# Linear attention and MLP in one kernel: the first block's reciprocals all transposed by DMA, in a new order of all engines

## The chip, the cores and the metric

The kernel runs on one core of a Trainium2 chip. The metric is the device time of one execution in microseconds (us); lower is better. A profile shows one execution: TensorE matmuls (PE) and weight loads (PEld), VectorE (DVE), ScalarE (ACT), GpSimd (POOL), and the queue of SyncE (SP or SPq), which issues every data transfer of this kernel.

## The reference

`x` is 2048 rows by 512 columns in bf16. An attention block with 32 heads of 16 and a two-layer MLP follow each other, each behind a layer norm and each added to its input:

```python
qkv = _layernorm(x) @ wqkv                       # 512 -> 3*512
phi = lambda t: jnp.where(t > 0, t + 1, jnp.exp(t)) + 1e-6
kv  = jnp.einsum("bhsd,bhse->bhde", phi(k), v)   # per head, over all rows
z   = jnp.einsum("bhsd->bhd", phi(k))
num = jnp.einsum("bhqd,bhde->bhqe", phi(q), kv)
den = jnp.einsum("bhqd,bhd->bhq", phi(q), z)[..., None] + 1e-6
h   = x + (num / den) @ wo
h2  = h + relu(_layernorm(h) @ w1) @ w2          # 512 -> 1792 -> 512
```

## The kernel before

The rows are cut into 16 tiles of 128, and four tiles make a block of 512 rows (blocks 0 to 3). A text, ORDER, lists every step of the kernel as a word, such as `K.8.0`. The words are issued one after the other, and each engine executes its own words in that order; semaphores are set from what each word reads and writes. So a word's place decides what it stands behind on its engine, and nothing is rescheduled later. The last number of a PE word is mostly the bank of the accumulator `bk` (8 banks) that it writes.

The words that matter, with their lines in the kernel before:

- `lx`, `lk`, `lq`, `lv`, `lo`, `l1`, `l2` (L201, L204): loads of the input and of the weights, issued by SP. `l1` and `l2` move 896 KB each.
- `S`, `A`, `R`, `N` (L222 to L250): layer norm of an input tile into `h_nat`, on DVE, with `R` (two activations) on ACT. `T` and `E` (L266, L276): transposing tiles 0 to 3 on PE and copying them to `lnT` on ACT. `X` (L287): transposing the other tiles by a DMA that SP issues.
- `K`, `Q` (L295, L303): the k and q products, four matmuls each. `F`, `U`, `M`, `D` (L313, L316, L320, L323): exp and relu on ACT, minimum and sum on DVE, which make phi. `W` (L328) takes the place of `U` and `D`: one DVE instruction that reads the accumulator itself. `qF` ... `qW` are the same for q.
- `G` (L347): a tile's share of phi(k) transposed times the normed input, into four banks; after 16 tiles `gA` (ACT, L380) or `gD` (DVE, L383) copy them to `gT`. `z`, `zc`, `zh`: the sums over phi(k). `kv`, `kx`, `m`, `mA` (L388 to L403): the product with the v weights, the mask, the product with `wo`.
- `dn` (L444): the denominators of a block, 16 small matmuls. `dnl` (L450) and `dnx` (L457): logarithm and exp(-x) on ACT, which give the reciprocals by row in `rn` (the buffer of the k weights, `wk_sb`, once these are used up).
- `dt` (L476): a reciprocal tile transposed by DMA into `rd`. `rt` and `re` (L266, L468): the same by four PE transposes and a copy on ACT. In the kernel before, tile 3 goes by `rt.3.3` and `re.3`, and all other tiles by `dt`.
- `dm` (L480): phi(q) times reciprocals into `pqs`, on DVE, one word for half a block. It needs all four tiles of the block's `rd`; and the `dt` of the next block, which write the same `rd`, wait for both `dm` words of this one.
- `h`, `hD`, `s`, `a`, `n` (L490, L496, L224, L225, L254): attention output of a tile, residual, second layer norm. `x` (L288): that tile transposed by DMA into `lnT`.
- `p`, `pA`, `pD` (L506, L512, L517): first MLP product and relu on ACT or DVE; each `p` word reads all four tiles of its block's `lnT`. `f`, `fo`, `fd` (L526, L534, L541): second MLP product, scaling with residual, store.

All DMAs share one queue and eight semaphores in turn: each DMA waits until the one eight places ahead of it has landed.

Of the kernel before, what the change touches and what calls it, by code (L numbers as in the profile page):

```python
# [15 lines left out]


ORDER = """
const table lx.0.1 lx.2.1 S.0 lx.1.1 S.2 A.0 S.1 A.2 R.0.1 N.0 R.2.1 lx.3.1 lk.0.2 lx.4.2 warm.1.7 warm.9.7
A.1 R.1.1 T.0.6 S.3 N.2 N.1 A.3 E.0 lk.2.2 warm.1.7 R.3.1 S.4 T.2.7 lx.6.2 E.2 N.3 S.5 T.1.4 A.4 K.0.1 E.1 A.5  # L20
F.0.1 R.4.2 S.6 T.3.2 K.1.0 M.0.1 E.3 U.0.1 lx.8.4 K.2.3 F.1.1 N.5 masks U.1.1 N.4 S.7 D.0.1 M.1.1 A.7 A.6
R.6.2 D.1.1 K.3.2 F.2.1 F.3.1 U.2.1 U.3.1 S.9 N.6 lx.12.4 X.5 G.0 X.4 G.1 M.2.1 A.9 S.8 N.7 A.8 M.3.1 D.2.1
R.8.2 K.5.1 lq.0.2 D.3.1 N.9 K.4.0 F.4.2 X.6 S.13 N.8 X.7 G.2 A.13 S.12 M.4.2 X.9 A.12 G.3 U.4.2 R.12.2 K.6.2
X.8 D.4.2 K.7.3 N.12 S.10 S.11 N.13 G.4 K.9.1 K.8.0 F.6.2 U.6.2 A.11 M.6.2 A.10 X.12 R.10.2 D.6.2 X.13 N.11
S.15 N.10 A.15 za.2 U.8.2 F.8.2 S.14 M.8.2 A.14 G.5 G.6 G.7 X.11 K.12.0 X.10 K.13.1 K.11.3 R.14.2 lq.2.2 za.4
N.14 D.8.2 K.10.2 N.15 za.6 X.14 F.12.2 U.12.2 X.15 F.10.2 G.8 Q.0.0.0 Q.0.1.1 M.12.2 lv.2.2 l1.0.2 l1.2.2
lo.0.4 lv.0.2 U.10.2 K.14.2 G.9 K.15.3 D.12.2 M.10.2 za.8 D.10.2 qU.0.0.2 G.10 za.10 qF.0.0.2 F.14.2 qM.0.0.2
za.12 Q.0.2.0 Q.0.3.1 G.11 M.14.2 zf.12 qF.0.2.2 G.12 W.14.2 qM.0.2.2 l2.7.7 qD.0.0.2 G.13 z.1.2.14 z.3.2.14
z.2.2.14 z.0.2.14 zc qW.0.2.2 G.14 G.15 zh dn.0.0 dnl.0 dnx.0.0.2 gD.2.2 gD.0.2 Q.1.0.2 Q.1.1.3 Q.1.3.1 kv.2.4
kv.3.4 dnx.0.3.1 dnx.0.2.1 kv.1.4 kv.0.4 Q.1.2.0 kx qF.1.0.2 qU.1.0.2 m.0.4 rt.3.3 m.2.6 m.1.5 Q.2.0.2 m.3.7  # L30
dt.1 qM.1.0.2 qF.1.2.2 dt.0 dt.2 re.3 qD.1.0.2 Q.2.1.3 mA.0.2 qM.1.2.2 l2.0.7 mA.2.2 qW.1.2.2 dn.1.5 dm.0.0.2
Q.2.3.1 dnl.1 dnx.1.0.2 dm.0.2.2 h.3.5 hD.3 dnx.1.2.2 qF.2.0.2 qU.2.0.2 s.3 h.1.4 hD.1 a.3 s.1 h.0.5 Q.2.2.0
n.3 hD.0 dt.5 dt.6 h.2.4 qU.2.2.2 qF.2.2.2 a.1 s.0 dt.7 hD.2 n.1 s.2 a.0 n.0 dt.4 dm.1.0.2 Q.3.0.2 Q.3.1.3
Q.3.3.1 Q.3.2.0 dm.1.2.2 a.2 x.3 h.4.6 h.7.4 qU.3.0.2 qF.3.0.2 x.1 h.6.5 h.5.7 qF.3.2.2 n.2 qM.2.2.2 qM.2.0.2
qD.2.0.2 qM.3.0.2 qD.2.2.2 x.0 dn.2.3 x.2 dnl.2 dnx.2.2.2 p.0.0.2 p.0.1.3 hD.4 qM.3.2.2 qW.3.2.2 qD.3.0.2
pD.0.0.2 hD.7 hD.5 dnx.2.0.2 p.0.3.1 dn.3.6 p.0.2.0 dt.10 dt.11 hD.6 s.5 s.4 dt.8 dt.9 p.0.5.3 p.0.4.2
dm.2.2.2 s.7 a.7 dm.2.0.2 r.0.4 pA.0.2.2 dnl.3 pA.0.4.2 p.0.7.1 p.0.6.0 dnx.3.2.2 pA.0.6.2 p.0.13.3 f.0.4.0.7
p.0.12.2 pA.0.12.2 f.1.5.0.7 h.9.3 h.10.1 h.11.0 h.8.6 dnx.3.0.2 a.4 s.6 hD.9 a.5 a.6 hD.10 hD.11 p.0.9.3
p.0.11.1 p.0.8.2 p.0.10.0 dt.14 dt.13 dt.15 f.3.7.0.7 pA.0.10.2 pA.0.8.2 n.5 dt.12 n.6 dm.3.0.2 dm.3.2.2 n.4
s.11 n.7 hD.8 h.14.1 h.13.3 f.0.4.7.7 h.12.0 h.15.6 hD.14 s.10 s.8 s.14 hD.12 s.9 x.5 x.7 x.6 x.4 f.1.5.7.7  # L40
f.3.7.7.7 fo.0 hD.15 p.1.9.1 p.1.8.0 f.2.6.0.7 pA.1.8.2 f.2.6.7.7 p.1.0.0 p.1.1.1 fo.1 a.14 a.10 a.8 fo.3 s.12
a.11 a.12 s.15 a.15 n.11 hD.13 s.13 a.13 a.9 n.8 n.10 p.1.3.3 n.9 n.12 pA.1.0.2 fo.2 x.10 fd.3 x.9 x.8 x.11
p.1.10.6 p.1.4.0 p.1.7.5 fd.0 p.1.5.1 p.1.2.2 p.1.11.7 p.1.6.4 n.14 pD.1.6.2 r.12.4 pA.1.4.2 n.15 n.13
pD.1.10.2 pA.1.2.2 p.2.4.0 p.2.5.1 pA.2.4.2 x.15 f.5.5.0.7 p.2.0.0 p.2.1.1 p.2.2.2 p.2.3.3 pA.2.0.2 p.1.13.1
f.7.7.0.7 p.1.12.0 f.4.4.0.7 pD.2.2.2 pD.1.12.2 p.2.7.3 p.2.6.2 p.2.13.1 f.6.6.0.7 f.7.7.7.7 f.5.5.7.7
p.2.12.0 r.4.4 pD.2.6.2 p.2.10.2 f.6.6.7.7 pA.2.12.2 x.12 x.14 x.13 fd.1 fd.2 p.2.9.1 p.2.11.3 p.2.8.0 fo.7
pA.2.10.2 pD.2.8.2 f.4.4.7.7 p.3.3.3 p.3.9.1 p.3.8.0 fo.4 pA.3.8.2 fo.5 fo.6 f.8.4.0.7 p.3.5.1 p.3.4.0 p.3.2.2
f.9.5.0.7 pD.3.4.2 pD.3.2.2 fd.5 fd.4 p.3.0.0 f.10.6.0.7 f.9.5.7.7 f.10.6.7.7 p.3.6.2 p.3.7.3 p.3.1.1 fd.6
f.8.4.7.7 pD.3.6.2 pA.3.0.2 r.8.4 fo.9 fo.10 p.3.13.1 f.11.7.0.7 p.3.11.3 p.3.12.0 pA.3.12.2 fo.8 f.11.7.7.7
fd.7 fd.9 p.3.10.2 f.12.4.0.7 f.14.6.0.7 fo.11 pD.3.10.2 f.15.5.0.14.3.1 f.12.4.7.7 f.14.6.7.7 fd.8 fd.10  # L50
fd.11 fo.15.3.1 fo.12 fo.14 f.13.5.0.7 f.13.5.7.7 fo.13 f.15.7.0.14.0.2 fd.12 fd.14 fd.13 fd.15.3.1
f.15.4.0.14.2.1 fo.15.0.2 fd.15.0.2 fo.15.2.1 fd.15.2.1
"""


# [521 lines left out]
```

## Time and profile before

| what | value |
|---|---|
| median of 3 runs | 170.41 us (170.32 to 170.6) |
| the profiled execution | 171.34 us |
| its span in the trace | 169.6 us |
| granted TensorE clock | 1.0 |

The profiled execution is 0.93 us above the median, and 1.74 us of it lie outside the span. The span is what the views of the trace divide; a saving in it is taken over to the median as it stands.

### The profile page before, as it was taken

Reading aid. Unit: us, or ns where it says so; the run is one execution under the profiler, and the core shown is the slowest. Engines: PE = TensorE matmul, PEld = TensorE weight load, DVE = VectorE, ACT = ScalarE, POOL = GpSimd, SP = SyncE. Lnnn points to the kernel's source line nnn. Section 1 sums busy time; section 2 is a strip of 40 time slices with the busy share of each in tenths; the row PEclk is TensorE's granted clock in tenths of the full one; section 3 lists DMA queues with packets and bytes.
Section 4 is the critical chain, followed back from the end, with each engine's and each line's share of the span. In section 5 each row is a group of like instructions: output and inputs, shape, how many; then the busy total and the mean of one; then the engine's idle time right before and its main releaser. Section 6 shows DMA issues by size and latency. Waiting matters only on the chain.

```text
span 169.6 us, 2272 instructions
## 1 busy us (share of the span) xinstructions
PE 162.6 (96%) x847; PEld 75.6 (45%) x863; DVE 102.6 (61%) x203; ACT 65.2 (38%) x98; POOL 4.9 (3%) x21
## 2 busy tenths in 40 slices
...
GB/s 128 312 192 142 110 81 125 270 395 261 65 122 203 108 64 66 62 31 95 60 69 0 9 115 62 69 120 1 0 0 0 124 0 4 0 93 31 0 66 62
DMA packets 31675, 15.75 MB, mean 93 GB/s; under 512 B 24240, under 2 KB 30640, under 8 KB 31664
## 3 DMA queue, kind: packets, MB, share of 16 engines
...
q8 instruction: 7, 0.11, 0.3%
q14 instruction: 4, 0.03, 0.1%
HBM read 7.86 MB, written 2.10 MB: 59 GB/s over the span
## 4 chain that ended last, share of the span: by engine, by line
PE 83%; DMA 7%; DVE 5%; SPq 2%; issue 2%; ACT 0%; DVEq 0%
PE bk L526 28%; PE bk L506 28%; PE bk L490 9%; PE bk L303 6%; PE bk L347 6%; PE bk L295 4%; DMA x_nat<-in_A_x_dram 3%; DMA lnT<-h_nat 2%; DVE st L222 2%; DMA rd<-wk_sb 2%; SPq L201 1%; DVE h_nat L247 1%; DVE eb L320 1%; PE bk L444 1%; PE bk L388 1%
## 5 line engine op out<-in xcount | busy, mean ns | idle before, releaser
L526 PE MATMUL bk<-w_sb,at 128*128 128x512 bf16 (+2 forms) x248 | 51.2, 355 | 0.2
L506 PE MATMUL bk<-lnT,w_sb 128*128 128x512 bf16 x220 | 50.9, 380 | 0.2
L512 ACT ACTIVATE at<-bk 128x1024 bf16<-128x1024 f32 x17 | 17.2, 1022 | 67.3 <-PE bk L506 60.9
L526 PEld LDWEIGHTS <-at 128*128 128x128 bf16 x252 | 23.5, 98 | 25.2
L506 PEld LDWEIGHTS <-w_sb 128*128 128x128 bf16 x224 | 21.7, 98 | 26.0
L517 DVE TENSOR_SCALAR at<-bk 128x1024 bf16<-128x1024 f32 x11 | 13.4, 1223 | 32.7 <-PE bk L506 32.6
L534 DVE SCALAR_TENSOR_TENSOR gT<-bk,rstd,h_nat 128x512 bf16<-128x512 f32 (+2 forms) x18 | 12.0, 688 | 15.9 <-PE bk L526 14.8
L313 ACT ACTIVATE eb<-bk 128x1024 bf16<-128x1024 f32 (+1 forms) x18 | 16.4, 924 | 4.0 <-PE bk L295 2.4
L295 PE MATMUL bk<-wk_sb,lnT 128*128 128x512 bf16 x63 | 15.3, 380 | 0.7 <-DMA lnT<-h_nat 0.5
L490 PE MATMUL bk<-m_sb,pqs 128*128 128x512 bf16 x61 | 15.1, 380 | 0.2
L303 PE MATMUL bk<-lnT,wq_sb 128*128 128x512 bf16 x61 | 14.6, 379 | 0.1
L496 DVE TENSOR_TENSOR h_nat<-bk,x_nat 128x512 bf16<-128x512 f32 x16 | 10.8, 684 | 4.7 <-PE bk L490 4.7
L316 ACT ACTIVATE rb<-bk 128x1024 bf16<-128x1024 f32 (+1 forms) x14 | 12.5, 901 | 2.6 <-PE bk L303 1.9
L347 PE MATMUL bk<-at,h_nat 128*128 128x512 bf16 x56 | 13.4, 379 | 0.1
L222 DVE BATCH_NORM_STATS2 st<-x_nat 128x6 f32<-128x512 bf16 x16 | 10.7, 677 | 3.1 <-DMA x_nat<-in_A_x_dram 3.1
L224 DVE BATCH_NORM_STATS2 st<-h_nat 128x6 f32<-128x512 bf16 x16 | 10.7, 682 | 0.1
L347 PEld LDWEIGHTS <-h_nat 128*128 128x128 bf16 x64 | 6.2, 98 | 8.7 <-issue 1.5
L490 PEld LDWEIGHTS <-pqs 128*128 128x128 bf16 x64 | 5.9, 98 | 8.7 <-DVE pqs L480 2.0
L295 PEld LDWEIGHTS <-lnT 128*128 128x128 bf16 x64 | 6.0, 98 | 8.3 <-DMA lnT<-h_nat 1.4
L303 PEld LDWEIGHTS <-wq_sb 128*128 128x128 bf16 x64 | 6.1, 97 | 6.9
L457 ACT ACTIVATE wk_sb<-ld 128x1024 bf16<-128x1024 f32 (+1 forms) x9 | 8.2, 951 | 0.1
L480 DVE TENSOR_TENSOR pqs<-pqT,rd 128x1024 bf16<-128x1024 bf16 x8 | 5.2, 685 | 4.4 <-DMA rd<-wk_sb 2.6
...
## 6 DMA issues: line engine op xcount, KB each, us to landing
w_sb<-in_B_w_dram SPq DMA_DIRECT2D x4, 896.0 KB, 5.8
...
```

The source lines that it names most:

```text
L222: op_S = lambda t: nc.vector.bn_stats(out=st[:, t, :], in_=x_nat[:, t, :])
L295: nc.tensor.matmul(bk[:, b, :], lhsT=lnT[c][:, kd, j * P : (j + 1) * P], rhs=wk_sb[:, kd, :], start=(kd == 0), stop=(kd == KD - 1),)
L303: nc.tensor.matmul(bk[:, b, :], lhsT=wq_sb[:, kd, j * P : (j + 1) * P], rhs=lnT[c][:, kd, :], start=(kd == 0), stop=(kd == KD - 1),)
L313: nc.scalar.activation(out=buf(eb, kind, i, n), in_=bank(at_bank[kind, i], n), func=ACT.Exp)
L316: nc.scalar.activation(out=buf(rb, kind, i, n), in_=bank(at_bank[kind, i], n), func=ACT.Relu)
L347: nc.tensor.matmul(bk[:, KD + kd, :], lhsT=ln_nat[:, t, kd * P : (kd + 1) * P], rhs=pk(t)[:, 0, :], start=(t == 0), stop=(t == NT - 1),)
L490: nc.tensor.matmul(bk[:, b, :], lhsT=pqs[:, (c * KD + jb) % NQ, j * P : (j + 1) * P], rhs=m_sb[:, jb, :], start=(jb == 0), stop=(jb == KD ...
L506: nc.tensor.matmul(bk[:, b, cols], lhsT=w1_sb[:, kd, f * P : (f + 1) * P], rhs=lnT[c][:, kd, cols], start=(kd == 0), stop=(kd == KD - 1),)
L512: nc.scalar.activation(out=acts[c % 2][:, f : f + n, :], in_=bank(at_bank["p", c, f], n), func=ACT.Relu)
L517: nc.vector.tensor_scalar(out=acts[c % 2][:, f : f + n, :], in0=bank(at_bank["p", c, f], n), scalar1=0.0, scalar2=None, op0=ALU.max,)
L526: nc.tensor.matmul(bk[:, b, 0 : w * P], lhsT=acts[c % 2][:, f, j * P : (j + 1) * P], rhs=w2_sb[:, f, k * P : (k + w) * P], start=(f == 0), ...
L534: nc.vector.scalar_tensor_tensor(out=o_t[:, t % NO, cols], in0=bk[:, at_bank["f", t, k], 0 : w * P], scalar=rstd2[:, t : t + 1], in1=h_nat ...
```

## The change

The set of computations is the same. The words differ in these points:

- `rt.3.3` and `re.3` are gone, and `dt.3` is added: all four reciprocal tiles of block 0 go by DMA. The two words `dnx.0.3.1` and `dnx.0.2.1` become one, `dnx.0.2.2`.
- `W.14.2` becomes `U.14.2` and `D.14.2`; `qW.0.2.2` becomes `qU.0.2.2` and `qD.0.2.2`; `gD.0.2` becomes `gA.0.2`; `lv.2.2` and `lv.0.2` become one load `lv.0.4`.
- Fourteen relu words change sides, eight from DVE to ACT (`pD.0.0.2` becomes `pA.0.0.2`) and six from ACT to DVE, and many `T`, `K` and `h` words get another bank.
- All the rest is order. A new function, `op_warmq`, is defined, and no word calls it.

The diff, cut to the first third of the order and the new function:

```diff
-const table lx.0.1 lx.2.1 S.0 lx.1.1 S.2 A.0 S.1 A.2 R.0.1 N.0 R.2.1 lx.3.1 lk.0.2 lx.4.2 warm.1.7 warm.9.7
-A.1 R.1.1 T.0.6 S.3 N.2 N.1 A.3 E.0 lk.2.2 warm.1.7 R.3.1 S.4 T.2.7 lx.6.2 E.2 N.3 S.5 T.1.4 A.4 K.0.1 E.1 A.5
-F.0.1 R.4.2 S.6 T.3.2 K.1.0 M.0.1 E.3 U.0.1 lx.8.4 K.2.3 F.1.1 N.5 masks U.1.1 N.4 S.7 D.0.1 M.1.1 A.7 A.6
-R.6.2 D.1.1 K.3.2 F.2.1 F.3.1 U.2.1 U.3.1 S.9 N.6 lx.12.4 X.5 G.0 X.4 G.1 M.2.1 A.9 S.8 N.7 A.8 M.3.1 D.2.1
-R.8.2 K.5.1 lq.0.2 D.3.1 N.9 K.4.0 F.4.2 X.6 S.13 N.8 X.7 G.2 A.13 S.12 M.4.2 X.9 A.12 G.3 U.4.2 R.12.2 K.6.2
-X.8 D.4.2 K.7.3 N.12 S.10 S.11 N.13 G.4 K.9.1 K.8.0 F.6.2 U.6.2 A.11 M.6.2 A.10 X.12 R.10.2 D.6.2 X.13 N.11
...
-za.12 Q.0.2.0 Q.0.3.1 G.11 M.14.2 zf.12 qF.0.2.2 G.12 W.14.2 qM.0.2.2 l2.7.7 qD.0.0.2 G.13 z.1.2.14 z.3.2.14
-z.2.2.14 z.0.2.14 zc qW.0.2.2 G.14 G.15 zh dn.0.0 dnl.0 dnx.0.0.2 gD.2.2 gD.0.2 Q.1.0.2 Q.1.1.3 Q.1.3.1 kv.2.4
-kv.3.4 dnx.0.3.1 dnx.0.2.1 kv.1.4 kv.0.4 Q.1.2.0 kx qF.1.0.2 qU.1.0.2 m.0.4 rt.3.3 m.2.6 m.1.5 Q.2.0.2 m.3.7
-dt.1 qM.1.0.2 qF.1.2.2 dt.0 dt.2 re.3 qD.1.0.2 Q.2.1.3 mA.0.2 qM.1.2.2 l2.0.7 mA.2.2 qW.1.2.2 dn.1.5 dm.0.0.2
-Q.2.3.1 dnl.1 dnx.1.0.2 dm.0.2.2 h.3.5 hD.3 dnx.1.2.2 qF.2.0.2 qU.2.0.2 s.3 h.1.4 hD.1 a.3 s.1 h.0.5 Q.2.2.0
...
+lx.0.1 const table lx.2.1 lx.1.1 lx.3.1 S.0 S.2 A.0 R.0.1 S.1 N.0 A.1 A.2 warm.9.7 warm.1.7 T.0.4 R.1.1 lk.0.2
+lx.4.2 warm.1.7 lk.2.2 lx.6.2 S.3 N.1 R.2.1 E.0 A.3 N.2 lx.8.4 S.4 T.1.7 T.2.4 S.5 E.1 A.4 A.5 R.3.1 K.0.7 N.3
+E.2 R.4.2 T.3.4 K.1.6 S.7 U.0.1 F.0.1 N.4 S.6 E.3 M.0.1 N.5 A.7 A.6 F.1.1 R.6.2 U.1.1 lx.12.4 K.2.2 K.3.3
+D.0.1 X.4 S.8 N.6 M.1.1 S.9 A.8 G.0 K.4.0 X.5 lq.0.2 X.6 A.9 D.1.1 N.7 U.2.1 F.2.1 U.3.1 K.5.1 R.8.2 F.3.1
+F.4.2 M.2.1 G.1 X.7 U.4.2 N.9 D.2.1 S.12 S.13 S.11 N.8 A.12 G.2 X.9 K.6.2 M.3.1 M.4.2 A.11 A.13 D.4.2 D.3.1
+K.7.3 R.12.2 N.12 F.6.2 S.10 M.6.2 A.10 N.13 K.9.1 G.3 S.14 U.6.2 R.10.2 X.8 X.12 D.6.2 N.10 X.13 G.4 K.8.0
...
+F.14.2 qM.0.0.2 za.12 zf.12 M.14.2 qF.0.2.2 qU.0.2.2 D.14.2 G.11 G.12 Q.1.1.3 z.0.2.14 z.2.2.14 z.3.2.14
+z.1.2.14 qM.0.2.2 qD.0.0.2 G.13 qD.0.2.2 zc zh dn.0.0 dnl.0 G.14 G.15 dnx.0.0.2 Q.1.0.2 gA.0.2 dnx.0.2.2
+Q.1.2.0 qU.1.0.2 qF.1.0.2 dt.0 gD.2.2 kv.1.4 kv.3.4 kv.2.4 kv.0.4 kx qM.1.0.2 Q.1.3.1 qF.1.2.2 m.0.4 m.2.6
+m.1.5 m.3.7 Q.2.1.3 qD.1.0.2 qM.1.2.2 qW.1.2.2 Q.2.0.2 mA.0.2 dt.1 dt.3 dt.2 l1.2.2 dm.0.0.2 mA.2.2 dm.0.2.2
+dn.1.5 dnl.1 Q.2.2.0 h.3.4 dnx.1.0.2 h.1.6 hD.3 s.3 hD.1 h.0.5 Q.2.3.1 dnx.1.2.2 qU.2.0.2 qF.2.0.2 dt.5 hD.0
...
+    def op_warmq(n, b):
+        for _ in range(n):
+            nc.tensor.matmul(bk[:, b, 0:P], lhsT=zeros[:, 0:P], rhs=zeros[:, 0:P], start=True, stop=True)
```

SP's own words after the last `X`, in the kernel before and in the changed one:

```
before: lv.2.2 l1.0.2 l1.2.2 lo.0.4 lv.0.2 l2.7.7 dt.1 dt.0 dt.2 l2.0.7 dt.5 dt.6 dt.7 dt.4 x.3 x.1 x.0 x.2 dt.10
        dt.11 dt.8 dt.9 dt.14 dt.13 dt.15 dt.12 x.5 x.7 x.6 x.4 x.10 fd.3 ...
after:  l1.0.2 lo.0.4 dt.0 dt.1 dt.3 dt.2 l1.2.2 dt.5 dt.6 dt.4 dt.7 x.3 x.1 x.0 x.2 l2.0.7 dt.8
        dt.11 dt.9 dt.10 l2.7.7 dt.12 x.5 x.7 x.6 x.4 dt.15 dt.14 dt.13 x.10 fd.1 ...
```

PE's own words from the first MLP product to the first one of block 1:

```
before: p.0.0.2 p.0.1.3 p.0.3.1 dn.3.6 p.0.2.0 p.0.5.3 p.0.4.2 p.0.7.1 p.0.6.0 p.0.13.3 f.0.4.0.7 p.0.12.2 f.1.5.0.7
        h.9.3 h.10.1 h.11.0 h.8.6 p.0.9.3 p.0.11.1 p.0.8.2 p.0.10.0 f.3.7.0.7 h.14.1 h.13.3 f.0.4.7.7 h.12.0 h.15.6
        f.1.5.7.7 f.3.7.7.7 p.1.9.1
after:  p.0.0.2 p.0.1.3 p.0.2.0 p.0.3.1 p.0.5.3 p.0.4.2 dn.3.6 p.0.7.1 p.0.6.0 p.0.12.2 p.0.13.3 p.0.11.1 p.0.10.0
        p.0.9.3 h.10.6 h.9.7 p.0.8.2 h.11.4 f.3.7.0.7 f.0.4.0.7 h.8.5 f.0.4.7.7 f.3.7.7.7 p.1.3.3
```

46 lines of the change are left out of this document (23 added, 23 removed).

## The prediction

> **What bounds the kernel now.** I read the page first: the engines' shares and the chain that ended last; then the view by stretches (busy time and instructions of each engine, granted clock in the third column from the end).
>
> ```profile
> span 169.6 us, 2272 instructions
> PE 162.6 (96%) x847; PEld 75.6 (45%) x863; DVE 102.6 (61%) x203; ACT 65.2 (38%) x98; POOL 4.9 (3%) x21
> PE 83%; DMA 7%; DVE 5%; SPq 2%; issue 2%; ACT 0%; DVEq 0%
> ```
>
> ```profile
> 4.00:20.00 16.00, 14.32 (x72) 6.15 (x72) 14.78 (x46) 12.02 (x31) 1.95 (x7) 1.00 0.69 194
> 20.00:62.60 42.60, 41.73 (x255) 19.52 (x259) 38.35 (x72) 28.79 (x36) 0.00 (x0) 1.00 0.64 171
> 62.60:167.00 104.40, 103.78 (x522) 48.93 (x529) 47.99 (x83) 23.15 (x31) 0.00 (x0) 1.00 0.20 45
> ```
>
> PE is the bound, so another order wins only what PE idles. Behind 62.6 us that is 0.62 of 104.4 us; from 20 to 62.6 it is 0.87, in the head 1.7. The chain in order of time (start, us, what) names the places where another engine set the pace:
>
> ```profile
> 18.33 3.38 DMA lnT<-h_nat
> 21.71 0.05 issue
> 21.75 1.04 PE bk L295 x4
> ...
> 46.53 3.04 DMA rd<-wk_sb
> ...
> 49.66 0.70 DVE pqs L480
> ...
> 50.41 3.08 PE bk L490 x12
> ...
> 78.36 3.45 PE bk L506 x16
> ```
>
> Two gates stand there. `K.8` waits for the transpose `X.8`, issued at 18.33 and landed at 21.71. The first `h`, at 50.41, waits for `dm`, which waits for `dt.2` (46.53 to 49.57). A matmul of 512 columns costs 3.45/16 = 0.2156 us, a word of four 0.86.
>
> A third gate is almost hidden. SP's timeline (start, us, what), and the transposes' issue times (ns, minimum, median, maximum) and times to landing by the view of `rd`:
>
> ```profile
> 11.11 2.59 SPq L287 DMA_TRANSPOSE lnT<-h_nat  x2
> ...
> 14.42 11.20 SPq L287 DMA_TRANSPOSE lnT<-h_nat  x8
> ...
> 43.22 4.53 SPq L476 DMA_TRANSPOSE rd<-wk_sb  x3
> ...
> 51.03 5.13 SPq L476 DMA_TRANSPOSE rd<-wk_sb  x4
> 56.26 5.16 SPq L288 DMA_TRANSPOSE lnT<-hn  x4
> 64.32 14.93 SPq L476 DMA_TRANSPOSE rd<-wk_sb  x8
> ```
>
> ```profile
> L476 SPq DMA_TRANSPOSE rd<-wk_sb x15: 1189/1202/1983, 43.2 to 78.0; - x15
> ...
> DMA to landing us min/median/max: 2.4/2.4/4.0
> ```
>
> Four transposes take 5.13 us to issue, 1.28 each. `dt.5` goes at 51.03, behind the second `dm` (49.66 and two of 0.69); the last of the next eight, `x.2`, goes at about 60.2 and lands 2.45 later, at 62.65. From the landing of `dt.2` that is 13.1 us. PE's timeline has the first `p`, which reads what `x.2` writes, at just that time:
>
> ```profile
> 41.16 0.54 PE L444 MATMUL bk<-zhd,pqT 128*128 128x8 bf16 x16
> ...
> 46.22 0.39 PE L266 MATMUL bk<-ident,wk_sb 128*128 128x128 bf16 x4
> 46.44 0.60 PE L400 MATMUL bk<-wo_sb,kvbd 128*128 128x512 bf16 x2
> ...
> 48.81 0.67 PE L444 MATMUL bk<-zhd,pqT 128*128 128x8 bf16 x16
> ...
> 62.68 1.69 PE L506 MATMUL bk<-lnT,w_sb 128*128 128x512 bf16 x7
> ```
>
> So `p.0.0` starts earlier only if `dt.2` lands earlier. As PE hardly idles afterwards, the end follows `p.0.0`.
>
> **The change part by part.**
>
> *The head.* DVE's and PE's timelines:
>
> ```profile
> 9.88 0.69 DVE L222 BATCH_NORM_STATS2 st<-x_nat 128x6 f32<-128x512 bf16 x1 [1.19 <-DMA x_nat<-in_A_x_dram]
> ...
> 10.68 0.73 DVE L247 TENSOR_SCALAR h_nat<-x_nat,mv,rstd 128x512 bf16<-128x512 bf16 x2
> ```
>
> ```profile
> 12.39 1.89 PE L347 MATMUL bk<-pk_lo,h_nat 128*128 128x512 bf16 x7 [1.17 <-DVE pk_lo L323]
> ...
> 22.63 2.75 PE L347 MATMUL bk<-at,h_nat 128*128 128x512 bf16 x12
> ```
>
> Before, `N.5` and `N.4` follow a minimum at 10.68, and the first transpose goes at 11.11. Now `N.4` stands right behind the statistics that start at 9.88 with the load (0.6 to the next start, then 0.40): `X.4` goes at 10.9, 0.2 earlier, and all later `X` with it. `X.9`, before at 14.42 + 2 x 1.28 = 17.0, goes at 16.8 and lands at 19.25. PE has `K.9` now as the eighth word behind `G.0`, before as the tenth. `G.0` stays near 12.39: its sum `D.0` follows one more `N` in place of one `S`. Seven words of 0.86 end at 18.4, so `K.9` waits until 19.3, and `K.9 G.3 G.4 K.8` end at 22.75, where `G.5` starts: 22.63 before. The old gate is gone (`X.8`, at 18.1, lands at 20.55 and is needed at 21.9, so even 3.38 us are covered), and `X.9` is late next. Sum +0.1 us. Bounds: `K.9` without a wait -0.7; `X.9` with the 3.38 of `X.8` +1.0.
>
> *`dn.0` before `G.14 G.15`, `W` taken off DVE.* `dn.0` needs `zh`:
>
> ```profile
> 39.61 0.16 DVE L372 COPY z_sb<-bk 128x4 f32<-128x4 f32 x1 [0.22 <-PE bk L366]
> 39.69 1.22 DVE L328 SCALAR_TENSOR_TENSOR pqT<-bk,eb 128x1024 bf16<-128x1024 f32 x1
> 40.82 0.28 DVE L375 TENSOR_TENSOR zhd<-mask_h,z_sb 128x128 bf16<-128x128 bf16 x1
> ```
>
> `qW.0.2` (1.22) stood between `zc` and `zh`; without it `zh` ends near 40.0. `G.13` behind the `z` words ends at 40.3 on PE, and `dn.0` follows there, with the head's 0.1 at 40.4: 0.76 earlier than 41.16. The logarithm and the reciprocals hang on it, so the first `dt` goes at 43.22 - 0.76 = 42.46. The two `W` cost ACT an `U` each, about 0.9, before `dnl.0`; ACT was waiting there. `dnx.0.2.2` stands behind `gA.0.2`, two ACT words of some 1.0 each that start with `G.15` half done at about 42.3: ready at 44.4, while `dt.3` has its turn at 45.0. Covered by 0.6.
>
> *`dt.3` instead of `rt.3` and `re.3`.* PE loses 0.22 us of work (46.22 to 46.44). What follows it is `dn.1`, which needs `qW.1.2`:
>
> ```profile
> 46.10 1.02 ACT L313 ACTIVATE eb<-bk 128x1024 bf16<-128x1024 f32 x1
> ```
>
> ```profile
> 47.69 1.23 DVE L328 SCALAR_TENSOR_TENSOR pqT<-bk,eb 128x1024 bf16<-128x1024 f32 x1
> ```
>
> That is done at 48.92 before, and `dn.1` runs from 48.81, its later matmuls behind it. Nothing in this chain is shortened, so the 0.22 turns into a wait at `dn.1`: 0 on the path. The price is on SP: three transposes become four. `dt.2` is issued three steps behind the first, at 42.46 + 3 x 1.28 = 46.3 if nothing is stretched. Before, two steps took 46.53 - 43.22 = 3.31 instead of 2.56; with that 0.75 it goes at 47.05. It lands 2.45 later where nothing is in its way, 3.04 as before. So the landing is at 48.75, 49.5 or 50.1, against 49.57. I take the stretch and the usual 2.45, as the lateness fell on the first transposes most (one of 4.0 us) and the last is now one further behind: 49.5, or -0.1. At 48.75 DVE still has `qW` until 48.92 and PE gets to `h.3` only at 50.2 behind `dn.1` and one `Q`, so no more than 0.2 to 0.4 can come from it.
>
> By the Trainium skill, VectorE: DVE Perf Modes, The three transpose paths, TensorE takes 390 ns for a 128x128 block and the DMA 1309 ns, and its rule is to use TensorE where PSUM will do as the destination. Here four blocks kept PE 0.22 us and would go by one DMA of 1.20 us issue and 2.4 us landing; that this speaks against the change is the second rival's case.
>
> *Loads.* They come from this part of the page (KB, us to landing):
>
> ```profile
> w_sb<-in_B_w_dram SPq DMA_DIRECT2D x4, 896.0 KB, 5.8
> ```
>
> `l1.2.2`, issued behind `dt.2` at about 48, lands by 54 and is needed at 62.6. `l2.0.7` goes behind `x.2`, where SP waited for the next reciprocals until 64.32 anyway. `lv.0.4` goes at about 26.3, ahead of `X.15`; at the rate of 896 KB in 5.8 us or less it lands by 30.5 and `X.15` by 31, while PE has `K.15` at 32. All 0; without the cover up to 1.5 for `X.15`.
>
> *Behind `p.0.0`.* Block 1's first `p` comes 100 wide matmuls and a `dn` later, at 62.6 + 21.6 + 0.4 = 84.6. Its `x` words: eight steps took 14.93 us from 64.32, of which 4.7 were waits; with the same waits, four `dt`, `l2.7.7` (0.6) and `dt.12`, `x.5` to `x.4` put the last issue at 79.8, landing at 82.3. Spare 2.3 us, cost 0; beyond it each us late is lost. The relu words that change sides wait for PE on both engines (ACT and DVE are busy 23 and 48 of the last 104 us): 0.
>
> *Sum.* PE reaches `p.0.0` at the landing of `x.2`, 49.5 + 13.1 = 62.6, -0.1 us, or -0.3 where `dt.2` is not stretched. I take -0.2: span 169.4, the profiled execution 171.1, and as that one is 0.93 above the median, a median of 170.2 us.
>
> **The rivals.**
>
> *Quiet transposes.* No stretch, and `X.9` in time: `h.3` at PE's own pace 0.2 earlier, the waits behind it inside the `h` words gone too, the head even. -0.4 to -0.5, 169.95 us. For it: most transposes of L476 take 1202 ns and land in 2.4 us. Against it: all three of block 0 were late.
>
> *The fourth transpose in series.* The first `dt` is 0.76 earlier, but a step is 1.28. If `dt.2` takes 3.04 as before, it lands at 50.1, and `dm`, `dt.5` to `x.2` and `p.0.0` move by +0.5: 170.9 us; with 4.0 it is 51.05, +1.5, 171.9 us. It is slower from a landing of `dt.2` behind 49.6 on. For it: lateness is in the trace at this place; against it: the load that followed `dt.2` and the other traffic there are no heavier. I put it at 171.0.
>
> What is late could be instruction packets, of which the page has few:
>
> ```profile
> q8 instruction: 7, 0.11, 0.3%
> q14 instruction: 4, 0.03, 0.1%
> ```
>
> The Trainium skill, Runtime: NRT & Kernel Launch, Instruction fetch mechanics, says that an engine's instructions are refilled in blocks of 16 KiB (256 instructions) by its own DMA queue, a cost "mostly hidden". Seven packets of 0.11 MB agree in size; by that rule PE's blocks, with 8 instructions fewer in all, come at nearly the old times, and 45 us would hit the second and third `dt` rather than the last.
>
> *No gain at all.* Each gate is replaced by one at the same place: 170.4 us.
>
> **How the numbers follow.** Forecast 0.37 (170.2), quiet 0.27 (169.95), fourth in series 0.26 (171.0), nothing 0.10 (170.4). A measurement of this kernel tells 0.2%, 0.34 us, from no change: faster is below 170.07, slower above 170.75. Faster: 0.26 of the quiet case and 0.11 of the forecast's lower part, 0.37. Same: 0.26 + 0.01 + 0.10 = 0.37. Slower 0.26. The forecast's own range is 169.9 to 170.5. The range reaches to 169.6 (head without a wait) and 171.2, which leaves out the 4.0 us landing.
>
> **What would show it.** `p.0.0` in PE's timeline at 62.3 to 62.7, and the landing of `dt.2` 13.1 us ahead of it; no wait of `K.8`, one before `K.9`; a new wait of `dn.1` for DVE L328; no PE idle behind 62.6. I am wrong if the chain shows `rd` landing behind 50, a `K` waiting over 0.5 us for `lnT`, or PE waiting for `lnT` near 84.

## The result, and the profile after

| what | before | after |
|---|---|---|
| median of 12 runs each | 170.52 us (170.09 to 171.16) | 171.08 us (170.72 to 171.82) |
| ratio | | 1.0035, 95% [1.0019, 1.0052] |
| the profiled execution | 171.34 us, span 169.6 | 171.44 us, span 169.7 |

The changed kernel is slower by 0.2 to 0.5%. (Ratios here and below come from undisturbed runs alone and are not the quotients of the medians beside them.) The two profiled executions show only 0.1 us of it. The first one is 0.93 us above the median that was known then (170.41), the second 0.36 above its own: 0.10 + 0.93 - 0.36 = 0.67 us is the difference of those medians, 171.08 - 170.41. So by the clock of the two profiles most of the loss can't be seen. They caught an input load at different times, as the second profile of the kernel before will show, and places in them can be compared only when they are counted from that load.

The page of the kernel after, the span, the engines' shares and the shares of the chain that ended last:

```profile
span 169.7 us, 2282 instructions
PE 163.8 (97%) x859; PEld 75.7 (45%) x859; DVE 98.1 (58%) x200; ACT 69.2 (41%) x101; POOL 4.9 (3%) x21
PE 81%; DVE 7%; DMA 6%; ACT 3%; issue 1%; SPq 0%; DVEq 0%
```

Its view by stretches, with PE's busy time behind the length:

```profile
4.00:20.00 16.00, 14.79 (x71) 6.15 (x70) 15.30 (x47) 12.51 (x32) 1.94 (x7) 1.00 0.73 197
20.00:62.60 42.60, 42.02 (x260) 19.54 (x257) 35.84 (x69) 30.09 (x37) 0.00 (x0) 1.00 0.54 130
62.60:167.00 104.40, 104.23 (x524) 48.96 (x524) 45.42 (x80) 25.30 (x33) 0.00 (x0) 1.00 0.27 62
```

PE is recorded busier in every stretch, and the end is no earlier. These sums hold no saving: the profile of before lacks more matmul records (847 of 863 against 859, all, after). What counts is when `p.0.0` starts. The chain of waits of the kernel after, in order of time (start, us, what), has it:

```profile
10.38 3.08 DMA lnT<-h_nat
...
47.08 2.49 DMA rd<-wk_sb
...
60.20 2.44 DMA lnT<-hn
62.64 0.14 issue
```

`dt.2` goes at 47.08 and lands at 49.57, `x.2` lands at 62.64, 13.07 later. SP's timeline and PE's timeline of the kernel after (start, us, engine, line, what; in brackets the idle time before):

```profile
42.02 6.32 SPq L480 DMA_TRANSPOSE rd<-wk_sb  x4
...
51.05 5.12 SPq L480 DMA_TRANSPOSE rd<-wk_sb  x4
```

```profile
13.51 0.82 PE L299 MATMUL bk<-wk_sb,lnT 128*128 128x512 bf16 x3 [0.19 <-DMA lnT<-h_nat]
...
62.77 1.46 PE L510 MATMUL bk<-lnT,w_sb 128*128 128x512 bf16 x6 [0.21 <-DMA lnT<-hn]
```

DVE's, ACT's and PE's rows of the kernel after for `dm`, `dnx.1` and the first `h`:

```profile
49.69 1.29 DVE L484 TENSOR_TENSOR pqs<-pqT,rd 128x1024 bf16<-128x1024 bf16 x2 [1.10 <-DMA rd<-wk_sb]
```

```profile
49.59 2.00 ACT L461 ACTIVATE wk_sb<-ld 128x1024 bf16<-128x1024 f32 x2
```

```profile
50.44 0.60 PE L494 MATMUL bk<-m_sb,pqs 128*128 128x512 bf16 x2 [0.41 <-DVE pqs L484]
```

PE now waits 0.41 us for `dm` ahead of the first `h`; in the kernel before it stood at 50.41 without a wait.

`p.0.0` starts at 62.77, 0.09 behind the kernel before, and the span is 0.1 longer. Everything behind has one length: the span less the start of `p.0.0` is 106.9 both times, and 106.9 to 107.0 in all profiles of the experiments but after_rt3. There it is 107.4: the last matmul ends as far behind `p.0.0` as in the kernel after (104.28 us both times), and what follows it takes 0.4 longer. So the others can be read by their `p.0.0`.

### The profile page after: what moved, and what is told of

Same layout as the page of the kernel before. It is cut to its first block, busy times and chain, and to the rows that moved or that the text cites. A ratio compares the mean times of both kernels' runs of the same rounds, so it can differ in the third digit from the quotient of the medians.

```text
span 169.7 us, 2282 instructions
## 1 busy us (share of the span) xinstructions
PE 163.8 (97%) x859; PEld 75.7 (45%) x859; DVE 98.1 (58%) x200; ACT 69.2 (41%) x101; POOL 4.9 (3%) x21
## 4 chain that ended last, share of the span: by engine, by line
PE 81%; DVE 7%; DMA 6%; ACT 3%; issue 1%; SPq 0%; DVEq 0%
PE bk L510 29%; PE bk L530 29%; PE bk L351 8%; PE bk L299 6%; PE bk L494 5%; PE bk L307 4%; DMA lnT<-h_nat 2%; DMA rd<-wk_sb 1%; DMA lnT<-hn 1%; DVE h_nat L500 1%; DMA x_nat<-in_A_x_dram 1%; DVE pqs L484 1%; DVE st L226 1%; DVE st L228 1%; ACT eb L317 1%
## 5 line engine op out<-in xcount | busy, mean ns | idle before, releaser
L516 ACT ACTIVATE at<-bk 128x1024 bf16<-128x1024 f32 x19 | 19.2, 1022 | 67.3 <-PE bk L510 67.3
L510 PEld LDWEIGHTS <-w_sb 128*128 128x128 bf16 x224 | 21.8, 98 | 26.3 <-issue 0.4
L521 DVE TENSOR_SCALAR at<-bk 128x1024 bf16<-128x1024 f32 x9 | 11.0, 1218 | 27.3 <-PE bk L510 27.3
L320 ACT ACTIVATE rb<-bk 128x1024 bf16<-128x1024 f32 (+1 forms) x16 | 14.5, 912 | 3.4 <-PE bk L299 1.8
L307 PE MATMUL bk<-lnT,wq_sb 128*128 128x512 bf16 x64 | 15.3, 379 | 0.0
L351 PE MATMUL bk<-at,h_nat 128*128 128x512 bf16 x56 | 13.5, 379 | 0.0
L461 ACT ACTIVATE wk_sb<-ld 128x1024 bf16<-128x1024 f32 x8 | 8.2, 1050 | 0.7 <-DMA rd<-wk_sb 0.6
```

The source lines that it names most:

```text
L307: nc.tensor.matmul(bk[:, b, :], lhsT=wq_sb[:, kd, j * P : (j + 1) * P], rhs=lnT[c][:, kd, :], start=(kd == 0), stop=(kd == KD - 1),)
L320: nc.scalar.activation(out=buf(rb, kind, i, n), in_=bank(at_bank[kind, i], n), func=ACT.Relu)
L351: nc.tensor.matmul(bk[:, KD + kd, :], lhsT=ln_nat[:, t, kd * P : (kd + 1) * P], rhs=pk(t)[:, 0, :], start=(t == 0), stop=(t == NT - 1),)
L510: nc.tensor.matmul(bk[:, b, cols], lhsT=w1_sb[:, kd, f * P : (f + 1) * P], rhs=lnT[c][:, kd, cols], start=(kd == 0), stop=(kd == KD - 1),)
L516: nc.scalar.activation(out=acts[c % 2][:, f : f + n, :], in_=bank(at_bank["p", c, f], n), func=ACT.Relu)
```

## The experiments

Each ran in five rounds beside the kernel before on the same chip; the three groups ran on three chips, with medians of before of 170.58 (both kernels again, before_dt3, after_rt3), 171.19 (after_rt3b, the halves, before_G5) and 171.00 us (the rest). All edits are in the order. In the expectations, theory A holds that the first profile of the kernel before caught a late execution and that the fourth transpose costs time; the others are described in their texts.

**Both kernels again.** No edit. For the kernel before:

> The kernel before, unchanged, profiled a second time. The first profile of it was of an execution 0.93 us above its median. Theory A (that execution had late transposes, a usual one has not): the span is 168.6 to 169.0, X.8 lands by 20.9 and K.8 does not wait over 0.2 us, the last rd tile of block 0 lands at 48.8 to 49.2 and p.0.0 starts at 61.9 to 62.3. Theory B (the surplus lies outside the span or in the profiling): the span is 169.4 to 169.7 again, with X.8 at 21.7 and p.0.0 at 62.7. The median is 170.5 either way.

170.65 us, ratio 0.9996 [0.9965, 1.0027], span 168.9. DVE's and PE's timelines of this second profile of the kernel before:

```profile
9.15 0.69 DVE L222 BATCH_NORM_STATS2 st<-x_nat 128x6 f32<-128x512 bf16 x1 [0.51 <-DMA x_nat<-in_A_x_dram]
```

```profile
21.08 1.04 PE L295 MATMUL bk<-wk_sb,lnT 128*128 128x512 bf16 x4 [0.57 <-DMA lnT<-h_nat]
21.96 1.24 PE L347 MATMUL bk<-at,h_nat 128*128 128x512 bf16 x5
```

The statistics that wait for the load `lx.6.2` start at 9.15, in the first profile at 9.88. From there on everything stands 0.7 us earlier: `K.8` at 21.08 for 21.75, `G.5` at 21.96 for 22.63, the end at 168.9 for 169.6. The wait for `X.8` is still there, as the chain from load to `X.8` moves as one. So 0.7 of the 0.93 us above the median came with a load that landed late, at the start of the stage that the prediction costed. The chain of waits of this profile has a second surprise:

```profile
48.31 0.52 PE bk L444 x16
...
48.85 0.38 ACT ld L450
...
50.21 1.05 ACT wk_sb L457
51.26 0.26 SPq L476
...
59.48 2.42 DMA lnT<-hn
61.91 0.05 issue
```

Here the chain to `x.2` does not come from `dt.2` and `dm`. It comes from block 1's denominators: `dn.1`, `dnl.1` and the two words of `dnx.1`, of which the chain lists the second. ACT's and SP's timelines have both words, and the first transpose, `dt.5`, right behind the first of them (49.24 + 1.05 = 50.29):

```profile
49.24 2.00 ACT L457 ACTIVATE wk_sb<-ld 128x1024 bf16<-128x1024 f32 x2
```

```profile
50.33 5.13 SPq L476 DMA_TRANSPOSE rd<-wk_sb  x4
```

`dt.5` has two gates, the end of `dm`, which frees `rd`, and the first word of `dnx.1`, which gives the rows to be transposed. DVE's and ACT's timelines of the first profile of the kernel before have them:

```profile
49.66 1.29 DVE L480 TENSOR_TENSOR pqs<-pqT,rd 128x1024 bf16<-128x1024 bf16 x2 [0.74 <-DMA rd<-wk_sb]
```

```profile
49.91 2.00 ACT L457 ACTIVATE wk_sb<-ld 128x1024 bf16<-128x1024 f32 x2
```

`dm` is done at 50.95. Of the two words of `dnx.1` the first takes 1.05 (the chain above has such a word alone) and is done at 50.96. Both gates of `dt.5`, which went at 51.03, were level.

The changed kernel again:

> The changed kernel, unchanged, profiled a second time. Theory A: the four transposes in series hold p.0.0 in every execution: dt.2 lands at 49.3 to 49.7, p.0.0 at 62.5 to 62.9, median 171.1. Theory B: the same trace; the two kernels then differ by less than 0.2 us inside the span.

170.76 us, ratio 1.0007 [0.9983, 1.003]. Its profiled execution is the longest of its twelve (172.08 us, span 169.8). Its DVE and SP timelines and PE's:

```profile
8.61 0.69 DVE L226 BATCH_NORM_STATS2 st<-x_nat 128x6 f32<-128x512 bf16 x1
```

```profile
9.64 2.59 SPq L291 DMA_TRANSPOSE lnT<-h_nat  x2
```

```profile
13.65 0.60 PE L299 MATMUL bk<-wk_sb,lnT 128*128 128x512 bf16 x2 [1.05 <-DMA lnT<-h_nat]
...
22.30 1.03 PE L351 MATMUL bk<-at,h_nat 128*128 128x512 bf16 x4
```

The load was there before 8.61, 0.7 us ahead of the first profile of this kernel, and `X.4` was issued at 9.64 for 10.38. It landed at 13.61, 3.97 us later, and `K.4` waited 1.05 us for it; `G.5` at 22.30 is no earlier than the 22.25 of the first profile. Between issue and landing of `X.4` the 512 KB load `lx.12.4` was in the queue (landed at 12.97). A `K` that waits over 0.5 us for `lnT` was one of the prediction's signs of being wrong.

A third profile of the changed kernel, on another chip:

> The changed kernel, unchanged, for a third time, to size the loss against the same chip's runs of the kernel before. Theory L (the loss is a floor: the changed head cannot use an early input load, so its fastest executions are slower while its slow ones are not): the fastest span is 0.4 to 0.6 above the fastest of the kernel before, the median 0.1 to 0.4 above. Theory N (no difference, the first result was scatter): fastest and median spans within 0.15 of the kernel before.

171.26 us, ratio 1.0029 [1.0003, 1.0056], span 169.7. DVE's and PE's timelines:

```profile
9.67 0.69 DVE L226 BATCH_NORM_STATS2 st<-x_nat 128x6 f32<-128x512 bf16 x1 [0.73 <-DMA x_nat<-in_A_x_dram]
```

```profile
22.58 0.59 PE L351 MATMUL bk<-at,h_nat 128*128 128x512 bf16 x2
...
62.71 1.46 PE L510 MATMUL bk<-lnT,w_sb 128*128 128x512 bf16 x6 [0.29 <-DMA lnT<-hn]
```

The start of those statistics and of `G.5`, by the same rows of each profile (the next experiments' too), in us; then, counted from `G.5`, the end of `dm`, the end of the first word of `dnx.1`, the issue of `dt.5` and the start of `p.0.0`. The rest is the order behind `G.5`:

| head | rest | profile | statistics | `G.5` | between | `dm` | `dnx.1` | `dt.5` | `p.0.0` |
|---|---|---|---|---|---|---|---|---|---|
| old | old | before, first profile | 9.88 | 22.63 | 12.75 | 28.32 | 28.33 | 28.40 | 40.05 |
| old | old | before_again | 9.15 | 21.96 | 12.81 | 27.96 | 28.33 | 28.37 | 39.99 |
| old | old, `dt.3` | before_dt3 | 8.82 | 21.59 | 12.77 | 28.48 | 28.33 | 28.56 | 40.28 |
| old | new | headB_restA | 8.79 | 21.59 | 12.80 | 28.34 | 28.40 | 28.43 | 40.14 |
| new | old | headA_restB | 8.95 | 21.82 | 12.87 | 28.24 | 28.34 | 28.38 | 40.00 |
| new | new | after_third | 9.67 | 22.58 | 12.91 | 27.88 | 28.39 | 28.42 | 40.13 |
| new | new | after, first profile | 9.35 | 22.25 | 12.90 | 28.73 | 28.39 | 28.80 | 40.52 |
| new | new | after_lx6 | 8.77 | 22.02 | 13.25 | 28.63 | 28.38 | 28.71 | 40.41 |
| new | new | after_again | 8.61 | 22.30 | 13.69 | 28.72 | 28.38 | 28.80 | 40.52 |
| new | new, `rt.3` | after_rt3 | 9.23 | 22.23 | 13.00 | 27.54 | 28.84 | 28.87 | 40.58 |
| new | new, `rt.3` | after_rt3b | 8.77 | 22.09 | 13.32 | 27.53 | 28.38 | 28.42 | 40.11 |

The old head follows the load at 12.8 us. The new one follows it 0.1 later while the load is late (in the first profile `K.4` waits 0.19 us for `X.4`, and `K.9` 0.1 for `X.9`), and not below about 21.8. There `X.4` seems to wait its turn behind `lx.12.4`: in the nine profiles in which the first transpose took over 2.8 us to land, it landed 0.55 to 0.76 behind that load. An early load is worth less in the new order.

Behind `G.5`, `dt.5` goes 0.03 to 0.08 us behind the later of its two gates in every profile, and `p.0.0` 11.6 to 11.7 behind `dt.5`. The gate `dnx.1` stands at 28.33 to 28.40 in all but after_rt3, in both orders, so `dt.5` can't go earlier, whatever `dt.2` does. The gate `dm` comes earlier or later with the transposes, and where it is the later one it costs time. In three of the four profiles of the full new order it is, and `p.0.0` comes 0.4 to 0.5 later than in the old rest.

The spans of all executions agree with the new head's floor in their lower ends (us; the first row of the kernel after is that of the result):

```
                 runs  shortest  median  longest
before, group 1    35     168.2   168.8    170.4
before_again       12     168.2   168.9    170.6
after_again        12     168.8   169.0    169.8
before, group 3    30     168.4   169.3    171.3
after_third        12     168.8   169.45   170.4
after              12     168.8   169.25   169.8
```

The shortest are 0.4 to 0.6 apart, the medians 0.15 to 0.2 on the same chip. That the floor is made by `X.4` is not shown, since no execution of 168.8 of the full change was profiled.

**The fourth transpose alone.** The kernel before with block 0's tile 3 by DMA, nothing else moved:

```diff
-kx qF.1.0.2 qU.1.0.2 m.0.4 rt.3.3 m.2.6 m.1.5 Q.2.0.2 m.3.7 dt.1 qM.1.0.2 qF.1.2.2 dt.0 dt.2 re.3 qD.1.0.2
+kx qF.1.0.2 qU.1.0.2 m.0.4 m.2.6 m.1.5 Q.2.0.2 m.3.7 dt.1 qM.1.0.2 qF.1.2.2 dt.0 dt.3 dt.2 qD.1.0.2
```

> The kernel before with only the fourth transpose: rt.3 and re.3 taken out, dt.3 put ahead of dt.2. Here dn.0 is not earlier. Theory A: dt.2 lands one step of 1.28 us later than in the kernel before of the same call, p.0.0 and the end 0.6 to 1.3 later, median 171.1 to 171.8. Theory C: the median stays at 170.5 (0.2 us of PE work less).

171.70 us, ratio 1.0046 [1.0023, 1.0069]: a loss of 0.8 us by the ratio, 1.1 between the medians. The profiled execution is the shortest of its twelve (span 168.9, their median 169.7), so its rows show the order of things and not the loss. SP's timeline and the chain:

```profile
42.18 5.30 SPq L474 DMA_TRANSPOSE rd<-wk_sb  x4
```

```profile
46.27 2.42 DMA rd<-wk_sb
...
48.78 0.70 DVE pqs L478
```

This execution is 0.37 us ahead of before_again at the first `dt` (42.18 against 42.55), and `dm` starts at 48.78 where before_again has 48.63. So the lead is gone and 0.15 more: the fourth step in series costs 0.5 us at `dm`, even where `dt.2` lands in 2.42. As `dm` had 0.4 to spare before `dnx.1`, 0.3 of it is left at `p.0.0` (40.28 against 39.99 behind `G.5`).

**The four PE transposes put back into the changed kernel.** `rt.3.3` and `re.3` again, `dt.3` out, all else as after:

```diff
-qF.1.2.2 m.0.4 m.2.6 m.1.5 m.3.7 Q.2.1.3 qD.1.0.2 qM.1.2.2 qW.1.2.2 Q.2.0.2 mA.0.2 dt.1 dt.3 dt.2
+qF.1.2.2 m.0.4 rt.3.3 m.2.6 m.1.5 m.3.7 re.3 Q.2.1.3 qD.1.0.2 qM.1.2.2 qW.1.2.2 Q.2.0.2 mA.0.2 dt.1 dt.2
```

> The changed kernel with dt.3 taken out and rt.3, re.3 put back where the kernel before has them (behind m.0 on PE, behind m.3 in the order): three transposes in series instead of four, and nothing else changed. Theory A (the fourth transpose in series holds p.0.0): dt.2 lands one step, 1.2 us, earlier, p.0.0 0.4 to 0.6 earlier, median 170.5. Theory C (the loss is made in the head, before 23 us, or behind 63 us): dt.2 lands earlier but the median stays within 0.2 of 171.1.

171.67 us, ratio 1.006 [1.0039, 1.0081]: not the gain that was expected, but 0.9 us more than the changed kernel in this group (170.76). All engines' timeline of after_rt3 from 46 us on:

```profile
46.67 0.59 ACT L470 ACTIVATE rd<-bk 128x512 bf16<-128x512 bf16 x1
...
47.32 1.89 PE L305 MATMUL bk<-lnT,wq_sb 128*128 128x512 bf16 x8 [0.35 <-ACT rd L470]
...
48.49 1.28 DVE L482 TENSOR_TENSOR pqs<-pqT,rd 128x1024 bf16<-128x1024 bf16 x2
49.04 0.55 PE L446 MATMUL bk<-zhd,pqT 128*128 128x8 bf16 x16
...
50.02 2.00 ACT L459 ACTIVATE wk_sb<-ld 128x1024 bf16<-128x1024 f32 x2
51.10 1.19 SPq L478 DMA_TRANSPOSE rd<-wk_sb  x1
```

`dm` runs at 48.49, 1.20 us earlier than the 49.69 of the changed kernel, as it should. `dt.5` still goes at 51.10: `Q.2.1` uses the bank of `rt.3.3` and waits for the copy `re.3`, `dn.1` comes at 49.04, and `dnx.1` gives its first word at 51.07. The other gate holds. A whole microsecond won at `dt.2` and `dm` buys nothing. Of the 0.9 us the profile shows 0.4 behind the last matmul; the rest is not explained.

The same with the two `Q` words exchanged, so that no one waits for the bank at once:

```diff
-... m.3.7 re.3 Q.2.1.3 qD.1.0.2 qM.1.2.2 qW.1.2.2 Q.2.0.2 mA.0.2 dt.1 dt.2
+... m.3.7 re.3 Q.2.0.2 qD.1.0.2 qM.1.2.2 qW.1.2.2 Q.2.1.3 mA.0.2 dt.1 dt.2
```

> The changed kernel with rt.3 and re.3 back in place of dt.3 as in after_rt3, and Q.2.0 ahead of Q.2.1 on PE, so that Q.2.1 no longer stands still for re.3, which reads the same bank 3 (0.5 us in after_rt3). Theory A2 (dt.5 waits for the later of two things, the end of dm, which hangs on dt.2, and the reciprocals of block 1, which hang on dn.1): dt.2 lands at 47.6, dm ends by 49.9, dt.5 goes with the reciprocals at 50.5 to 50.7, p.0.0 at 62.1 to 62.3, median 0.4 to 0.5 below the changed kernel, 170.3 to 170.6. If the fourth transpose costs nothing (theory C): within 0.2 of the changed kernel.

171.53 us beside 171.19, ratio 1.0025 [1.0003, 1.0047]. Its ACT and SP timelines:

```profile
49.42 2.00 ACT L459 ACTIVATE wk_sb<-ld 128x1024 bf16<-128x1024 f32 x2
```

```profile
50.51 2.50 SPq L478 DMA_TRANSPOSE rd<-wk_sb  x2
```

`dt.5` goes at 50.51, behind `dnx.1` again, and `p.0.0` starts at 62.20. The places came as expected, the median did not fall below that of before. With the fourth transpose undone in either way, the rest of the change is still no gain.

**The change in halves**, cut at `G.5`. The head of before and the rest of after, then the head of after and the rest of before:

```diff
-... G.4 K.9.1 G.3 S.14 ... G.4 K.8.0 G.5 masks U.8.2        (head of after)
+... G.4 K.9.1 K.8.0 F.6.2 ... S.14 M.8.2 A.14 G.5 X.10      (headB_restA)
```

> The order of the kernel before up to and with its word G.5, and from there the changed kernel's words in their order, less those already done. Theory H (the changed head is held by X.4, which lands at 13.5 behind the last input load, so that G.5 cannot start before 22.4, while the old head follows the input load and is at 21.6 to 22.0 in a usual execution) and theory A (four transposes in series hold dt.5): G.5 starts at 21.6 to 22.0, dt.2 still lands 1.45 ahead of dt.5, p.0.0 at 62.1 to 62.4, median 170.2 to 170.5, that is 0.4 to 0.6 below the changed kernel. Theory D (the loss is all behind G.5): G.5 earlier, but p.0.0 at 62.7 and the median within 0.2 of the changed kernel's 170.8 to 171.1.

171.25 us beside 171.19, ratio 1.002 [0.9992, 1.0048].

```diff
-... G.4 K.9.1 K.8.0 F.6.2 ... S.14 M.8.2 A.14 G.5 G.6       (head of before)
+... G.4 K.8.0 G.5 masks N.11 S.15 A.15 za.2 ... A.14 G.6    (headA_restB)
```

> The changed order up to and with its word G.5, and from there the words of the kernel before, less those already done. Theory H: G.5 at 22.4 in every execution, dt.5 at 50.7 to 50.9, p.0.0 at 62.3 to 62.5, median 170.9 to 171.1, with a floor of 170.5 instead of 169.9. Theory D: the median is that of the kernel before, 170.5 to 170.6, with a floor of 170.0.

171.17 us, ratio 0.9996 [0.9974, 1.0017]. Both intervals hold no change; the first holds the full loss of 1.0035 too, the second does not. Which half carries the 0.3% is not settled by the times; if one does, it is sooner the rest than the head. The places in their profiles are alike (`dt.5` at 50.02 and 50.20, `p.0.0` at 61.73 and 61.82), but both profiled executions are the shortest of their twelve.

**`G.5` ahead of `K.8` in the kernel before**, which gives PE work while `X.8` is on its way:

```diff
-S.11 N.13 G.4 K.9.1 K.8.0 F.6.2 U.6.2 ... S.14 M.8.2 A.14 G.5 G.6 G.7 X.11
+S.11 N.13 G.4 K.9.1 G.5 K.8.0 F.6.2 U.6.2 ... S.14 M.8.2 A.14 G.6 G.7 X.11
```

> The kernel before with one word moved: G.5 ahead of K.8 instead of behind it. In both profiles of the kernel before K.8 waits 0.7 us for X.8; G.5 needs only tile 5's phi(k), done by then. Theory H2 (the wait of K.8 is on the path): no wait of K.8 above 0.1, G.6 0.6 to 0.7 earlier, and 0.4 to 0.7 less in the end, median 169.9 to 170.2. Theory X (what is won there is lost again at p.0.0, which waits for x.2 behind dn.1, qW and two sets of transposes that do not move): G.6 earlier, p.0.0 and the median unchanged at 170.5 to 170.6.

170.68 us beside 171.19, ratio 0.999 [0.9962, 1.0018]: unclear. PE's timeline of before_G5:

```profile
20.33 1.03 PE L345 MATMUL bk<-at,h_nat 128*128 128x512 bf16 x4
21.19 1.03 PE L293 MATMUL bk<-wk_sb,lnT 128*128 128x512 bf16 x4
22.05 1.24 PE L345 MATMUL bk<-at,h_nat 128*128 128x512 bf16 x5
...
62.05 2.76 PE L504 MATMUL bk<-lnT,w_sb 128*128 128x512 bf16 x12
```

No PE wait for `X.8` is left, and `p.0.0` is at 62.05, where before_again has 61.95. PE's wait in the head was taken away, and PE waits further on instead: 0.30 us for ACT at 24.24 and 0.42 for `dm` at 49.80.

**The load `lx.6.2` a place earlier**, ahead of the second half of the k weights, in both kernels:

```diff
-E.0 lk.2.2 warm.1.7 R.3.1 S.4 T.2.7 lx.6.2 E.2        (before_lx6)
+E.0 lx.6.2 warm.1.7 R.3.1 S.4 T.2.7 lk.2.2 E.2
-lx.4.2 warm.1.7 lk.2.2 lx.6.2 S.3                     (after_lx6)
+lx.4.2 warm.1.7 lx.6.2 lk.2.2 S.3
```

> The kernel before with two loads exchanged: the input tiles 6 and 7 (lx.6.2) ahead of the second half of the k weights (lk.2.2). Theory L: lx.6.2 lands some 0.7 us earlier (8.0 to 8.8), DVE's statistics of tile 6 and the first DMA transpose go earlier by as much, and the median falls by 0.2 to 0.6. If the head does not follow this load: no change within 0.15; if the k weights, now landing 0.7 later, hold K.0 to K.3: slower.

173.12 us beside 171.00, ratio 1.0126 [1.0085, 1.0166], span 171.5. PE's timeline of before_lx6, and its view by stretches beside that of before_again (granted clock third from the end):

```profile
9.84 0.61 PE L293 MATMUL bk<-wk_sb,lnT 128*128 128x512 bf16 x2 [2.02 <-DMA wk_sb<-in_A_wqkv_dram]
10.27 0.61 PE L264 MATMUL bk<-ident,h_nat 128*128 128x128 bf16 x4
10.67 4.26 PE L293 MATMUL bk<-wk_sb,lnT 128*128 128x512 bf16 x12
```

```profile
10.00:13.50 3.50, 3.50 (x13) 1.56 (x12) 2.21 (x7) 2.84 (x7) 0.00 (x0) 0.54 0.44 164
```

```profile
10.00:13.50 3.50, 3.00 (x15) 1.28 (x14) 3.50 (x14) 2.67 (x8) 0.00 (x0) 1.00 0.58 163
```

`K.0` stops in its middle for 2.0 us until the weights land, and then the clock is granted at 0.54 until 13.5 us: twelve matmuls take 4.26 us and not 12 x 0.2156 = 2.6. `p.0.0` starts at 64.53. The rival, that the k weights would hold `K.0`, was right, and the price was more than the wait.

> The changed kernel with the same exchange. Theory L: lx.6.2 lands as much earlier, X.4 is issued earlier, but X.4 still lands at 13.0 to 13.6 behind the last input load (lx.12.4), K.4 starts there, and the median stays within 0.2 of the changed kernel's in this call. If the changed head follows lx.6.2 as the old one does: 0.3 to 0.6 faster.

Ratio 1.0063 [1.0028, 1.0099], with single runs from 171.11 to 175.56 and a median of 173.32 us over all twelve. Five of them have a granted clock of 0.998 to 1.0 and take 171.1 to 171.7; the seven at 0.98 to 0.99 take 173.0 to 175.6. Its profile is a short one (span 169.4): `lx.6.2` lands at 7.57, 1.75 ahead of the first profile of the changed kernel, and `X.4` lands at 13.33, 0.14 ahead. It stays behind `lx.12.4`, as in the table above.

> The kernel before with both small moves: lx.6.2 ahead of lk.2.2, and G.5 ahead of K.8. Theory L with the gate at x.2: no more than before_lx6 or before_G5 alone gives, 0.2 to 0.6 below the kernel before, as p.0.0 then waits for x.2. If both gains add: 0.8 to 1.0 below.

Both edits of before together, 171.38 us, ratio 1.0027 [1.0008, 1.0046]. `p.0.0` is at 62.41 in a profile at full clock: `K.0` waits 1.13 us for its weights, and `G.0` starts at 12.40, in before_again at 11.66. No version here is faster than the kernel before by more than its interval.

## Why the prediction was wrong

Its places in the trace came nearly all as forecast by the clock; its time did not. The agreement of the places hides a miss.

- *`dt.2` at 49.5, `x.2` 13.1 later, `p.0.0` at 62.6.* Measured: 49.57, 13.07 and 62.77. But the forecast was made for a load whose statistics start at 9.88, and in the profile of the kernel after they start 0.53 earlier, at 9.35. With 0.53 added, `G.5` (22.78 for 22.75), `dn.0` (40.48 for 40.4) and the first `dt` (42.55 for 42.46) came as forecast, and then the landing of `dt.2` 0.6 later (50.10 for 49.5) and `p.0.0` 0.7 later (63.30 for 62.6). That both agree by the clock is luck.
- *"I take the stretch and the usual 2.45 ... 49.5, or -0.1"*, the price of the fourth transpose. This step failed. The stretch of the transposes was taken at 0.75 us and was 47.08 - 42.02 - 3 x 1.28 = 1.22. From the statistics to `p.0.0` the kernel before takes 52.80 us in both its profiles, the changed one 53.42: a loss of 0.62 (0.15 in the head, 0.47 behind `G.5`) where a gain of 0.2 was forecast, and the medians are 0.56 to 0.67 apart. The stretch has no fixed size: in the other profiles of the new rest it was 0.99, 0.38, 0.82 and 1.01.
- *"So `p.0.0` starts earlier only if `dt.2` lands earlier."* True and not enough, and why no gain came even where the stretch was small: `dt.5` has a second gate, `dnx.1`, and the profile of before had it at 50.96, level with `dm`. The wait of `dn.1` that the prediction put at "0 on the path" is on that second path. In after_third the stretch was 0.38 and `dm` was done 0.44 earlier behind `G.5` than in the kernel before, and `dt.5` went no earlier (28.42 against 28.40). after_rt3 landed `dt.2` 1.95 us earlier (47.62) and `p.0.0` stood at 62.81.
- *The head, +0.1.* The size was right where the load is late (12.9 against 12.8 us behind it), and in part by the gate that was forecast: `X.9` landed at 18.74 and held `K.9` by 0.1. `K.4`, which waited for `X.4`, was not forecast. With an early load the loss is up to 0.9 us (13.69), which a sum made on one late profile could not show.
- *"that one is 0.93 above the median, a median of 170.2"*. The surplus was a late load: 0.73 us of it at the statistics (9.88 against 9.15) and 0.7 at the end. To take it off is right as long as both kernels follow the load alike. With the loss of 0.62 in place of the gain it gives 171.34 + 0.62 - 0.93 = 171.03, near the 171.08 measured. That is an estimate from one pair of profiles: by after_third (53.04) the loss is 0.24, by after_again (54.21) 1.41, of which 0.9 in the head.
- *The waits.* `K.8` has none, `dn.1` waits 0.2 us for DVE L332, and PE has no idle time behind 62.8: as forecast. The wait of 0.41 for `dm` at the first `h` was not. `l1.2.2`, `l2.0.7`, `lv.0.4` and the relu words held no one.
- *The rivals.* The fourth transpose in series, put at 171.0, with `dt.2` landing at 50.1 and `p.0.0` 0.5 later, comes nearest in number and in mechanism, and before_dt3 shows its cost alone (1.0046). But undoing it in the changed kernel (after_rt3, after_rt3b) brings no gain, so it is not the whole cause: two gates stand at one place, the later decides, and the new head is not touched by it. The quiet transposes did not come: landings in block 0 took 2.5 to 4.3 us.
- *Instruction packets.* The traces bear the suspicion out as far as a coincidence can. In the kernel after a packet of 16 KB starts at 43.94, within the issue of the second `dt` (43.26, 2.47 us long), and in the kernel before at 45.07, within the issue that took 1.98. Over the fourteen profiles one of 8 or 16 KB starts between issue and landing in 30 of the 42 transposes whose issue took over 1.4 us, and in 133 of the other 566. No run moved a packet, so that they cause the stretch is not shown.
- *The Trainium skill's rule*, VectorE: DVE Perf Modes, Rules for kernel authors, to use TensorE where a destination in PSUM will do, agrees with before_dt3 (slower by 0.2 to 0.7%), and not with after_rt3, where the four blocks on PE cost a wait for their bank (0.35 us there) and nothing was won.

What stays open: how the 0.3% divides. The traces show a loss in the head with an early load and one at `dm` with stretched transposes; how often each comes is not measured. The three comparisons of the full change gave 1.0035, 1.0007 and 1.0029, the halves 1.002 and 0.9996 with intervals that hold 1.
